# Transposing q of the last two batches by DMA instead of on the matrix engine, with a new order of units

## Chip, cores, metric

The kernel runs on one core of one Trainium2 chip. The metric is the device time of one execution in microseconds (us). Ratios below are between runs of the fast state alone. Medians and ranges are over all runs, slow ones included, as recorded; leaving out the slow ones moves no median by more than 0.2 us. A ratio is the mean time of one kernel's fast runs over the mean time of the fast runs of the kernel before in the same rounds on the same chip, so it is not quite the ratio of the medians that stand beside it.

Names: PE is the matrix engine (PEld its weight loads), DVE the vector engine, ACT the scalar engine, POOL GpSimd, SP the engine whose queue issues most stores and small copies. A profile line "L289" means line 289 of that kernel's source; the change shifts lines, so the q transposes are L289 before and L295 after, the spatial matmuls L473 and L494, the attends L381 and L402, the V projection L414 and L435, the output projection L514 and L535.

## The reference

Four batches, eight heads, 768 positions, head size 64. A small matrix per head mixes blocks of k and v; q, mixed k and mixed v go through attention inside blocks of 96; then a gated MLP with a spatial mixing matrix follows.

```
P      = five rounds of exp and row/column normalisation of sort_net     # [b, h, 8, 8]
k_sort = einsum('bhij,bhjcd->bhicd', P, k_blocks)                        # same for v
attn   = softmax(q_block @ k_sort_block.T / sqrt(64))                    # 96 x 96 per block
x      = attn @ v_sort_block                                             # heads side by side: [b, 768, 512]
h      = relu(x @ w_in);  u, v = halves of h
v_n    = layer-normalised v
gated  = u * (w_spatial @ v_n + b_spatial)
out    = gated @ w_out
```

## The kernel before

The whole program is a fixed list of short units, issued in list order on every engine. One token is a unit, its index, its batch, the engine that empties its PSUM tile (A for ACT, D for DVE), and which of four PSUM tiles it uses. `q11A2` is: transpose heads 4 to 7 of q of batch 1, in PSUM tile 2, copied out by ACT.

```python
UNITS = {"v": "vmix", "k": "ktr", "q": "qtr", "s": "score", "z": "sums", "a": "attend",
         "t": "vtr", "B": "vblk",
         "X": "vstart", "V": "vproj", "N": "norm", "U": "uproj", "S": "spatial", "O": "oproj"}
```

The q unit is 24 transposes on PE and one copy:

```python
def qtr(self, n, eng, ps):
    t = ps_tile(ps, BF16)
    qT = qk_pool.tile([128, 2, S], BF16, name="qT", tag="q", bufs=3)
    for x in range(2):
        hp = 2 * n + x
        for g in range(G):                       # G = 6
            for hh in range(2):
                nc.tensor.transpose(t[hh * 64:hh * 64 + 64, x, g * 128:(g + 1) * 128],
                    q_in[self.b][:, 2 * hp + hh, g * D:(g + 1) * D], ident_bf)
        self.q[hp] = qT[:, x, :].rearrange("p (g i t) -> p i g t", g=G, i=NB)
    copy(eng, qT, t[:, :, 0:S])
```

The v unit mixes v of one pair of heads. After both pairs of one half (heads 0 to 3, or 4 to 7) are done, eight small DMA copies bring that half into the block layout that the attends read. This part is not touched by the change, but the argument ends up here:

```python
def vmix(self, hp, eng, ps):
    # two matmuls into PSUM, copy to self.vm ... (cut)
    self.mixed.append(hp)
    if hp ^ 1 in self.mixed:                     # both pairs of this half are there
        for i in range(NB):                      # 8 copies of 48 KB on the SP queue
            nc.sync.dma_start(
                out=self.vb[:, i, half].rearrange("c h d -> c (h d)"),
                in_=self.vm[i * TB:(i + 1) * TB, half].rearrange("t g h d -> t g (h d)"))
```

The loads of batch b+1 are released by the first score of batch b, from GpSimd: v, then k, then q.

The softmax here doesn't subtract the row's maximum and nothing guards it: scores larger than these inputs give would overflow.

Of the kernel before, what the change touches and what calls it, by code (L numbers as in the profile page):

```python
# [9 lines left out]
BF16 = mybir.dt.bfloat16  # L10
# [6 lines left out]
def _raw_ap(base_ap: bass.AP, off_delta: int, dims) -> bass.AP:  # L17
    return bass.AP(
        tensor=base_ap.tensor,
        offset=base_ap.offset + off_delta,  # L20
        ap=[list(d) for d in dims],
    )
# [8 lines left out]
def kernel(  # L31
# [12 lines left out]
    nc = tc.nc  # L44

    B, H, S, D = q.shape
    NB = sort_net.shape[-1]
    BLK = S // NB
    G = S // 128
# [7 lines left out]
    HP = H // 2  # L57
# [5 lines left out]
    pd_pool = ctx.enter_context(tc.tile_pool(name="pd", bufs=B))  # L63
    ld = ctx.enter_context(tc.tile_pool(name="ld", bufs=2))
    att = ctx.enter_context(tc.tile_pool(name="att", bufs=2))
    qk_pool = ctx.enter_context(tc.tile_pool(name="qk", bufs=7))
    ex_pool = ctx.enter_context(tc.tile_pool(name="ex", bufs=8))
    xt_pool = ctx.enter_context(tc.tile_pool(name="xt", bufs=4))
    ln_pool = ctx.enter_context(tc.tile_pool(name="ln", bufs=3))
# [9 lines left out]
    def ps_tile(n, dt=FP32):  # L79
        return psum.tile(  # L80
            [128, 2, 512 if dt == FP32 else 1024], dt, name=f"ps{n}", tag=f"ps{n}",
        )
# [7 lines left out]
    b_nat = pers.tile([128, S], FP32)  # L90

    def load_heads(x, b, name):
        t = ld.tile([128, H, G * D], BF16, name=name, tag=name)
        nc.gpsimd.dma_start(  # L94
            out=t,
            in_=_raw_ap(x, b * H * S * D, [[G * D, 128], [S * D, H], [1, G * D]]),
        )
        return t

    v_in, k_in, q_in = {}, {}, {}  # L100
# [8 lines left out]
        out=a16.rearrange("p (j t) -> p j t", t=TB),  # L109
        in_=a16.rearrange("p (j t) -> p j t", t=TB),  # L110
# [6 lines left out]
        out=sel.rearrange("p i (j t) -> p i j t", t=TB),  # L117
        in_=sel.rearrange("p i (j t) -> p i j t", t=TB),
# [14 lines left out]
        out=w_in_sb.rearrange("p (j x) f -> p j (x f)", x=2),  # L133
        in_=moe_w_in.rearrange("(j p x) f -> p j (x f)", j=2, x=2),
# [20 lines left out]
    def sinkhorn():  # L155
        for n in range(5):
            nc.scalar.activation(out=p_all, in_=p_all, func=AF.Exp)
            nc.vector.reduce_sum(out=rowsum, in_=p_all, axis=AX.X)
            nc.vector.reciprocal(out=rowsum, in_=rowsum)
            nc.vector.tensor_mul(  # L160
                out=p_all, in0=p_all, in1=rowsum.to_broadcast([BH, NB, NB]),
            )
            nc.vector.reduce_sum(
                out=colsum, in_=p_all.rearrange("p i j -> p j i"), axis=AX.X,
            )
            nc.vector.reciprocal(out=colsum, in_=colsum)
            nc.vector.tensor_mul(
                out=p_all if n < 4 else p_bf, in0=p_all,
                in1=_raw_ap(colsum, 0, [colsum.ap[0], [0, NB], colsum.ap[1]]),
            )  # L170

    def warm(n, ps):
        t = ps_tile(ps)
        for _ in range(n):
            nc.tensor.matmul(t[:, 0, :], lhsT=ident_bf, rhs=warm_sb, start=True, stop=True)
# [5 lines left out]
    def make_pdiag(b, eng, h0, n, src=None):  # L181
        base = h0 if src is not None else b * NB * H + h0
        src = prep_sb if src is None else src
        eng.tensor_mul(
            out=pdiag[b][:, h0:h0 + n],
            in0=_raw_ap(mask16, 0, [mask16.ap[0], [0, n], [TB, NB], [1, TB]]),
            in1=_raw_ap(src, base, [src.ap[0], [1, n], [H, NB], [0, TB]]),
        )
# [5 lines left out]
    def transpose_p():  # L194
        for x in range(2):
            nc.vector.transpose(
                out=p_t[:, x, :], in_=p_bf[:, x * (NB // 2):(x + 1) * (NB // 2), :].rearrange("p i j -> p (i j)"),
            )
# [24 lines left out]
    def wsp_unit(gs, eng, ps):  # L223
        tp = ps_tile(ps, BF16)
        for go in range(G):
            nc.tensor.transpose(
                tp[:, 0, go * 128:(go + 1) * 128],
                wsp_nat[:, go, :].rearrange("p (s g) -> p g s", g=G)[:, gs, :],
                ident_bf,
            )  # L230
        copy(eng, wspT[:, gs, :], tp[:, 0, 0:S])

    def copy(eng, out, in_):
        if eng is nc.scalar:
            nc.scalar.copy(out=out, in_=in_)  # L235
        else:
            nc.vector.tensor_copy(out=out, in_=in_)
# [10 lines left out]
    class Attention:  # L248
# [7 lines left out]
        def vmix(self, hp, eng, ps):  # L256
# [18 lines left out]
            if hp ^ 1 in self.mixed:  # L275
                for i in range(NB):
# [2 lines left out]
                        in_=self.vm[i * TB:(i + 1) * TB, half].rearrange("t g h d -> t g (h d)"),  # L279
                    )  # L280

        def qtr(self, n, eng, ps):
            t = ps_tile(ps, BF16)
            qT = qk_pool.tile([128, 2, S], BF16, name="qT", tag="q", bufs=3)
            for x in range(2):
                hp = 2 * n + x
                for g in range(G):
                    for hh in range(2):
                        nc.tensor.transpose(  # L289
                            t[hh * 64:hh * 64 + 64, x, g * 128:(g + 1) * 128],  # L290
                            q_in[self.b][:, 2 * hp + hh, g * D:(g + 1) * D],
                            ident_bf,
                        )
                self.q[hp] = qT[:, x, :].rearrange("p (g i t) -> p i g t", g=G, i=NB)
            copy(eng, qT, t[:, :, 0:S])  # L295

        def mixed_t(self, src, hp, eng, ps):
            t = ps_tile(ps).rearrange("p x c -> p (x c)")
# [100 lines left out]
    class Gmlp:  # L399
# [122 lines left out]


    SCHEDULE = """
        k00A2 k10A3 k20D0 s10-1 s20-2 k30D3 s00-0 s30-1 t30D2 t10A3 t00D0 z10-1 t20D2 s40-3
        B10D1 B00D0 z00-2 B30D3 s60-1 a10-2 a00-0 B20D3 s50-1 s70-2 z20-1 X10-0 z30-3 a20-2
        a30-1 X00-3 V20-2 V10-- w30A1 V00-- U30A2 v11A0 v21A1 U20A3 w40D2 w10D0 N00-- U00A1
        v01A3 U10A2 w20D0 w50D1 w00A3 k11D2 k31A0 q01D1 k01A3 q11A2 k21A0 v31A1 S00-3 s01-2
        s11-0 S20-1 s51-3 s31-2 S10-0 z11-1 s21-3 S30-2 s61-1 a11-0 z01-3 a01-2 s71-1 s41-3
        O10D0 z31-1 z21-2 O00A3 a31-1 a21-0 O20D2 V01-3 v12D1 v02A0 V11-2 v32A3 V21-0 v22A2  # L530
        U01A1 k02A3 q12D0 k22A2 q02D1 k32A3 k12D0 U11D2 N01-- s42-1 s12-3 U21D0 s62-2 s02-1
        S01-3 s32-2 s72-1 S11-0 s52-3 s22-2 S21-1 z02-0 z22-3 U31D2 z32-0 a32-1 S31-3 a22-2
        z12-0 a12-1 a02-3 O21A0 O01D2 O11A1 V02-3 v13D0 v03A2 V12-1 v33A3 V22-2 v23A1 U02A0
        k03A3 q13D2 k23A1 q03D0 k33A3 k13D2 U12D1 N02-- s43-0 s13-3 U22D2 s63-1 s03-0 S02-3
        s33-1 s73-0 S12-2 s53-3 s23-1 S22-0 z03-2 z23-3 U32D1 z33-2 a33-0 S32-3 a23-1 z13-2  # L535
        a13-0 a03-3 O22A2 O02D1 O12A0 V03-3 V13-2 V23-1 N03-- U03A0 U13A3 U23A2 U33A1 S03-0
        S13-3 S23-2 S33-1 O03A0 O13A3 O23A2
    """
    UNITS = {
        "v": "vmix", "k": "ktr", "q": "qtr", "s": "score", "z": "sums", "a": "attend",  # L540
        "t": "vtr", "B": "vblk",
        "X": "vstart", "V": "vproj", "N": "norm", "U": "uproj", "S": "spatial", "O": "oproj",
    }
    with tc.manual_schedule(engines={ET.PE, ET.DVE, ET.Activation, ET.Pool}):
        attn = {b: Attention(b) for b in range(B)}
        gmlp = {}
        sinkhorn()
        warm(9, 1)
        attn[0].qtr(0, ACT, 2), attn[0].qtr(1, ACT, 3)
        warm(2, 1)  # L550
        transpose_p()
        spread(0, 1, 0), spread(1, 3, 1)
        for x in range(1, B):
            make_pdiag(x, nc.gpsimd, 0, H)
        nc.gpsimd.tensor_copy(
            out=b_bc.rearrange("p (g c) -> p g c", g=G),
            in_=b_nat.rearrange("p (c g) -> p g c", g=G),
        )
        for step in SCHEDULE.split():
            name, n, b = step[0], int(step[1]), int(step[2])  # L560
            eng = {"A": ACT, "D": DVE, "-": None}[step[3]]
            ps = None if step[4] == "-" else int(step[4])
            if name == "w":
                wsp_unit(n, eng, ps)
            elif name in "XVNUSO":
                if b not in gmlp:
                    gmlp[b] = Gmlp(b)
                if name == "S":
                    eng = DVE if b == B - 1 and len(gmlp[b].gt) == FC - 1 else nc.gpsimd
                getattr(gmlp[b], UNITS[name])(n, eng, ps)  # L570
            else:
                getattr(attn[b], UNITS[name])(n, eng, ps)
                if name == "s" and 1 <= b < B - 1 and len(attn[b].e) == 1:
                    gate = small.tile([1, 1], BF16, name="gate", tag="gate")
                    nc.gpsimd.tensor_copy(out=gate, in_=attn[b].e[n][0:1, 0, 0, 0:1])
                    v_in[b + 1] = load_heads(v, b + 1, "v_in")
                    k_in[b + 1] = load_heads(k, b + 1, "k_in")
                    q_in[b + 1] = load_heads(q, b + 1, "q_in")


# [28 lines left out]
```

## Time and profile before

| | kernel before |
|---|---|
| median, range | 158.89 us, 158.71 to 159.65 (3 runs) |
| profiled span, mean granted clock | 157.0 us, 0.998 |
| busy: PE, DVE, ACT, POOL | 142.9, 97.8, 92.4, 48.4 us |
| q units on PE | 8, of 24 transposes each |

PE is busy almost throughout. The measure that I use below is where the chain of PE work stands at fixed points: the start of the first q unit of batch 1, and the start of the first V unit of batches 1, 2 and 3 (V1, V2, V3). Between V1 and V2, and between V2 and V3, lies the same work of one whole batch, so the two distances are the price of a batch in PE time. Before they are 32.96 us each (V1 at 61.87, V2 at 94.83, V3 at 127.79 us). The lines of this profile that carry the bound stand in the prediction.

### The profile page before, as it was taken

To read this page: it belongs to the slowest core of one execution; us is meant where nothing else is said; L and a number is where in the kernel's file an instruction comes from. 1 tells how busy PE (TensorE), PEld (TensorE's weight loads), DVE (VectorE), ACT (ScalarE), POOL (GpSimd) and SP (SyncE) were. 2 spreads that over 40 slices of the span, in tenths; PEclk is the share of its full clock that TensorE was granted. 3 is DMA by queue.
4 is the path that set the end of the run, shared out by engine and by line. 5 is a ranking of instruction groups with operands and counts; after the bars stand their busy time and mean duration, and the time that the engine had idled before them with its cause. 6 is when DMAs were issued, how large, how long until landed. Compare 5 with 4: busy or idle time off the path is not lost.

```text
span 157.0 us, 4379 instructions
## 1 busy us (share of the span) xinstructions
PE 142.9 (91%) x1892; PEld 84.2 (54%) x1901; DVE 97.8 (62%) x197; ACT 92.4 (59%) x139; POOL 48.4 (31%) x47
## 2 busy tenths in 40 slices
PE   0967998979999999999999999999999999999960
PEld 0355884547865645467565544586556444666430
DVE  3777896487723566598944861999446837844510
ACT  3157977587894773597767326796564526640240
POOL 7975914000019920000757210000353400008400
PEclk9999999999999999999999999999999999999999
DMA  2999999999936999944599947045400063000064
GB/s 14 191 203 210 218 267 192 204 204 206 171 55 68 194 207 233 341 101 63 69 189 208 204 124 317 9 63 77 63 0 6 4 258 143 0 0 0 4 267 138
DMA packets 20964, 21.53 MB, mean 137 GB/s; under 512 B 1296, under 2 KB 18960, under 8 KB 20816
## 3 DMA queue, kind: packets, MB, share of 16 engines
q0 software_dynamic: 13504, 12.58, 49.8%
q1 hardware_dynamic: 7296, 8.53, 20.0%
q8 instruction: 15, 0.25, 0.6%
q10 hardware_dynamic: 144, 0.13, 0.3%
q14 instruction: 5, 0.04, 0.1%
HBM read 24.78 MB, written 6.29 MB: 198 GB/s over the span
## 4 chain that ended last, share of the span: by engine, by line
PE 66%; DMA 20%; POOL 5%; DVE 3%; issue 1%; POOLq 1%; DVEq 0%
DMA q_in<-in_q_dram 20%; PE ps L473 19%; PE ps L514 12%; PE ps L457 10%; PE ps L414 10%; PE ps L344 4%; PE ps L289 3%; DVE vs L484 2%; PE ps L301 2%; PE ps L381 2%; PE ps L260 2%; PE ps L363 1%; POOL v_in L94 1%; PE ps L500 1%; POOL k_in L94 1%
## 5 line engine op out<-in xcount | busy, mean ns | idle before, releaser
L485 POOL TENSOR_TENSOR gt<-vs,u_sb 128x768 bf16<-128x768 f32 x15 | 24.6, 1646 | 71.9 <-DVE vs L484 50.4
L473 PE MATMUL ps<-wspT,v_sb 128*128 128x384 bf16 x192 | 33.4, 327 | 0.0
L351 ACT ACTIVATE ex<-ps 96x768 bf16<-96x768 f32 x32 | 24.1, 803 | 9.5 <-PE ps L344 9.3
L484 DVE TENSOR_TENSOR vs<-ps,b_bc 128x768 f32<-128x768 f32 (+1 forms) x17 | 15.5, 911 | 21.0 <-PE ps L473 21.0
L473 PEld LDWEIGHTS <-v_sb 128*128 128x128 bf16 x192 | 17.9, 98 | 11.6
L457 PE MATMUL ps<-xt,w_in_sb 128*128 128x384 bf16 x128 | 23.0, 326 | 0.0
L436 DVE BATCH_NORM_STATS2 stats<-v_sb 128x6 f32<-128x512 bf16 x24 | 16.2, 674 | 10.1 <-ACT v_sb L241 10.1
L414 PE MATMUL ps<-w_in_sb,xt 128*128 128x512 bf16 x93 | 22.3, 379 | 0.2
L514 PE MATMUL ps<-w_out_sb,gt 128*128 128x512 bf16 x83 | 19.9, 380 | 0.4
L241 ACT ACTIVATE v_sb<-ps 128x1024 bf16<-128x1024 f32 (+1 forms) x15 | 12.4, 854 | 10.4 <-PE ps L414 10.4
L391 DVE TENSOR_TENSOR xt<-ps,lns 128x384 bf16<-128x384 f32 x32 | 15.7, 550 | 4.3 <-PE ps L381 3.3
L235 ACT COPY o_sb<-ps 128x1024 f32<-128x1024 f32 x7 | 7.1, 1012 | 18.0 <-PE ps L514 18.0
L457 PEld LDWEIGHTS <-w_in_sb 128*128 128x128 bf16 x128 | 12.0, 98 | 8.5 <-issue 0.6
L414 PEld LDWEIGHTS <-xt 128*128 128x128 bf16 x96 | 9.1, 98 | 10.6 <-DVE xt L391 0.4
L514 PEld LDWEIGHTS <-gt 128*128 128x128 bf16 x88 | 7.9, 98 | 10.3 <-POOL gt L485 1.2
L369 ACT ACTIVATE lns<-ps 128x384 f32<-128x384 f32 x16 | 7.8, 488 | 8.1 <-PE ps L363 8.0
L235 ACT CAST kT<-ps 128x768 bf16<-128x768 f32 x12 | 9.3, 803 | 1.8 <-PE ps L301 1.8
L344 PE MATMUL ps<-qT,kT 64*96 64x96 bf16 x256 | 9.7, 210 | 0.4 <-ACT kT L235 0.3
L344 PEld LDWEIGHTS <-kT 64*96 64x96 bf16 x256 | 7.2, 121 | 4.8 <-issue 3.7
L447 DVE TENSOR_SCALAR v_sb<-v_sb,mv,rstd 128x512 bf16<-128x512 bf16 x24 | 8.3, 417 | 0.6 <-ACT rstd L445 0.6
L370 ACT ACTIVATE lns<-lns 128x384 f32<-128x384 f32 x16 | 8.4, 523 | 0.5
L241 ACT ACTIVATE u_sb<-ps 128x768 bf16<-128x768 f32 x10 | 7.9, 811 | 1.2 <-PE ps L457 1.0
(78 smaller groups left out, 167.2 us busy)
## 6 DMA issues: line engine op xcount, KB each, us to landing
out_dram<-o_sb SPq DMA_DIRECT2D x11, 512.0 KB, 2.7
q_in<-in_q_dram POOLq DMA_DIRECT2D x4, 768.0 KB, 16.3
k_in<-in_k_dram POOLq DMA_DIRECT2D x4, 768.0 KB, 11.8
v_in<-in_v_dram POOLq DMA_DIRECT2D x4, 768.0 KB, 10.6
vb<-vm SPq DMA_DIRECT2D x48, 48.0 KB, 2.5
wsp_nat<-in_moe_w_spatial_dram POOLq DMA_DIRECT2D x1, 1152.0 KB, 21.6
w_in_sb<-in_moe_w_in_dram POOLq DMA_DIRECT2D x1, 1024.0 KB, 15.7
w_out_sb<-in_moe_w_out_dram POOLq DMA_DIRECT2D x1, 512.0 KB, 30.8
```

The costliest lines, as they stand in the source:

```text
L235: nc.scalar.copy(out=out, in_=in_)
L241: nc.scalar.activation(out=out, in_=in_, func=AF.Relu)
L344: nc.tensor.matmul(t[0:BLK, hh, ii * BLK:(ii + 1) * BLK], lhsT=self.k[hp][rows, i * BLK:(i + 1) * BLK], rhs=self.q[hp][rows, i], start=Tru ...
L351: nc.scalar.activation(out=e.rearrange("p h i c -> p h (i c)"), in_=t[0:BLK, :, 0:NB // 2 * BLK], func=AF.Exp, scale=scale,)
L391: nc.vector.tensor_mul(out=self.xt[j][:, dh, :].rearrange("p (g i t) -> p i g t", g=G, i=NB)[:, i0:i0 + NB // 2], in0=t[:, dh, 0:HW].rearr ...
L414: nc.tensor.matmul(self.vt[n][:, x, :], lhsT=self.xt(kc)[:, g * 128:(g + 1) * 128], rhs=w_in_sb[:, kc, DH:DFF], start=(kc == 0), stop=(kc ...
L436: nc.vector.bn_stats(out=stats, in_=v_sb[:, x, :])
L457: nc.tensor.matmul(t[:, x, 0:HW], lhsT=w_in_sb[:, kc, mc * 128:(mc + 1) * 128], rhs=self.xt(kc)[:, x * HW:(x + 1) * HW], start=(kc == 0), ...
L473: nc.tensor.matmul(t[:, x, 0:HW], lhsT=self.v[g][:, mc * 128:(mc + 1) * 128], rhs=wspT[:, g, x * HW:(x + 1) * HW], start=(g == 0), stop=(g ...
L484: nc.vector.tensor_add(out=vs[:, x], in0=t[:, x, 0:HW], in1=b2[:, x])
L485: eng.tensor_mul(out=gt2[:, x], in0=vs[:, x], in1=u2[:, x])
L514: nc.tensor.matmul(t[:, x, :], lhsT=self.gt[mc][:, g * 128:(g + 1) * 128], rhs=w_out_sb[:, mc, :], start=(mc == 0), stop=(mc == FC - 1),)
```

## The change

Intent: take the q transposes of batches 2 and 3 off PE. DVE puts q into pairs of heads in one copy, and one DMA on the SP queue transposes all 24 blocks of 128x128 a stage before they are needed. For this q of the next batch is loaded first, and the list of units was reordered. Some buffers changed too: q as loaded has one instead of two, and the transposed q lies in one tile for all four pairs of heads, with two buffers instead of three of half the size.

```diff
+        def qdma(self, n, eng, ps):
+            qr = qk_pool.tile([128, G, H, D], BF16, name="qr", tag="qr", bufs=1)
+            nc.vector.tensor_copy(
+                out=qr.rearrange("p g h d -> p h g d"),
+                in_=q_in[self.b].rearrange("p h (g d) -> p h g d", g=G),
+            )
+            nc.sync.dma_start(
+                out=self.q_tile().rearrange("p g x c -> p (g x) c"),
+                in_=qr.rearrange("p g h d -> p (g h d)"), transpose=True,
+            )
 ... (q_tile: one tile for the four pairs; qtr writes into it)
                     nc.gpsimd.tensor_copy(out=gate, in_=attn[b].e[n][0:1, 0, 0, 0:1])
+                    q_in[b + 1] = load_heads(q, b + 1, "q_in")
                     v_in[b + 1] = load_heads(v, b + 1, "v_in")
                     k_in[b + 1] = load_heads(k, b + 1, "k_in")
-                    q_in[b + 1] = load_heads(q, b + 1, "q_in")
```

The order, cut to batch 1 up to its first attends (before, then after):

```diff
-  V00-- U30A2 v11A0 v21A1 U20A3 w40D2 w10D0 N00-- U00A1 v01A3 U10A2 w20D0 w50D1 w00A3
-  k11D2 k31A0 q01D1 k01A3 q11A2 k21A0 v31A1 S00-3 s01-2 s11-0 S20-1 s51-3 s31-2 S10-0 z11-1
-  s21-3 S30-2 s61-1 a11-0 ...
+  V00-- v01A3 U20A1 v21D2 w20A0 N00-- U30A3 v31A1 U10A0 w30D2 w10A3 w00D1 v11A0
+  k01D2 k31A3 q01D1 k21A0 q11D2 k11D3 s01-1 S10-0 s71-2 s51-1 S20-3 s31-0 s61-2 S00-1 s11-3
+  s41-0 S30-2 s21-1 z11-3 Q02-- a11-0 ...
```

The new list moves two things that matter later. The v units stand in another order, and the first score of batch 1 (`s01`), which releases the loads of batch 2, now comes before the first spatial unit instead of after it.

Batches 2 and 3 are reordered likewise; the new unit `Q02` stands among the attends of batch 1, and `Q03` stands in batch 2 before its third spatial unit.

More of the change, by code (lines that the diff above doesn't have):

```diff
@@ L65 @@
     att = ctx.enter_context(tc.tile_pool(name="att", bufs=2))
-    qk_pool = ctx.enter_context(tc.tile_pool(name="qk", bufs=7))
+    qk_pool = ctx.enter_context(tc.tile_pool(name="qk", bufs=6))
     ex_pool = ctx.enter_context(tc.tile_pool(name="ex", bufs=8))
@@ L92, in load_heads @@
     def load_heads(x, b, name):
-        t = ld.tile([128, H, G * D], BF16, name=name, tag=name)
+        t = ld.tile([128, H, G * D], BF16, name=name, tag=name, bufs=1 if x is q else 2)
         nc.gpsimd.dma_start(
@@ L280, in vmix, with q_tile @@
                     )
+        def q_tile(self):
+            if not self.q:
+                qT = qk_pool.tile([128, G, HP, 128], BF16, name="qT", tag="q", bufs=2)
+                for hp in range(HP):
+                    self.q[hp] = qT[:, :, hp, :].rearrange("p g (i t) -> p i g t", i=NB)
+                self.qT = qT
+            return self.qT
         def qtr(self, n, eng, ps):
             t = ps_tile(ps, BF16)
-            qT = qk_pool.tile([128, 2, S], BF16, name="qT", tag="q", bufs=3)
             for x in range(2):
-                hp = 2 * n + x
                 for g in range(G):
@@ L290, in qtr @@
                             t[hh * 64:hh * 64 + 64, x, g * 128:(g + 1) * 128],
-                            q_in[self.b][:, 2 * hp + hh, g * D:(g + 1) * D],
+                            q_in[self.b][:, 4 * n + 2 * x + hh, g * D:(g + 1) * D],
                             ident_bf,
                         )
-                self.q[hp] = qT[:, x, :].rearrange("p (g i t) -> p i g t", g=G, i=NB)
-            copy(eng, qT, t[:, :, 0:S])
+            copy(
+                eng,
+                self.q_tile()[:, :, 2 * n:2 * n + 2, :].rearrange("p g x c -> p x g c"),
+                t[:, :, 0:S].rearrange("p x (g c) -> p x g c", g=G),
+            )
[8 more added lines that the diff above has]
+                in_=qr.rearrange("p g h d -> p (g h d)"), transpose=True,
+            )
         def mixed_t(self, src, hp, eng, ps):
@@ L524 @@
     SCHEDULE = """
-        k00A2 k10A3 k20D0 s10-1 s20-2 k30D3 s00-0 s30-1 t30D2 t10A3 t00D0 z10-1 t20D2 s40-3
-        B10D1 B00D0 z00-2 B30D3 s60-1 a10-2 a00-0 B20D3 s50-1 s70-2 z20-1 X10-0 z30-3 a20-2
-        a30-1 X00-3 V20-2 V10-- w30A1 V00-- U30A2 v11A0 v21A1 U20A3 w40D2 w10D0 N00-- U00A1
-        v01A3 U10A2 w20D0 w50D1 w00A3 k11D2 k31A0 q01D1 k01A3 q11A2 k21A0 v31A1 S00-3 s01-2
-        s11-0 S20-1 s51-3 s31-2 S10-0 z11-1 s21-3 S30-2 s61-1 a11-0 z01-3 a01-2 s71-1 s41-3
-        O10D0 z31-1 z21-2 O00A3 a31-1 a21-0 O20D2 V01-3 v12D1 v02A0 V11-2 v32A3 V21-0 v22A2
@@ L531 @@
-        U01A1 k02A3 q12D0 k22A2 q02D1 k32A3 k12D0 U11D2 N01-- s42-1 s12-3 U21D0 s62-2 s02-1
-        S01-3 s32-2 s72-1 S11-0 s52-3 s22-2 S21-1 z02-0 z22-3 U31D2 z32-0 a32-1 S31-3 a22-2
-        z12-0 a12-1 a02-3 O21A0 O01D2 O11A1 V02-3 v13D0 v03A2 V12-1 v33A3 V22-2 v23A1 U02A0
-        k03A3 q13D2 k23A1 q03D0 k33A3 k13D2 U12D1 N02-- s43-0 s13-3 U22D2 s63-1 s03-0 S02-3
-        s33-1 s73-0 S12-2 s53-3 s23-1 S22-0 z03-2 z23-3 U32D1 z33-2 a33-0 S32-3 a23-1 z13-2
-        a13-0 a03-3 O22A2 O02D1 O12A0 V03-3 V13-2 V23-1 N03-- U03A0 U13A3 U23A2 U33A1 S03-0
@@ L537 @@
-        S13-3 S23-2 S33-1 O03A0 O13A3 O23A2
+        k00A2 k10D3 k30D0 s00-1 s10-2 k20D3 s20-1 s30-0 t00D2 t10A3 t30D1 t20D0 z10-2 B00D3
+        s70-1 B10D2 s50-0 s40-3 z00-1 a10-2 a00-0 s60-3 B20D1 B30A2 z20-3 X10-0 z30-2 a20-1
+        a30-3 X00-2 V20-1 V10-- U00A3 w50A1 w40D0 V00-- v01A3 U20A1 v21D2 w20A0 N00-- U30A3
+        v31A1 U10A0 w30D2 w10A3 w00D1 v11A0 k01D2 k31A3 q01D1 k21A0 q11D2 k11D3 s01-1 S10-0
+        s71-2 s51-1 S20-3 s31-0 s61-2 S00-1 s11-3 s41-0 S30-2 s21-1 z11-3 Q02-- a11-0 z31-2
@@ new lines @@
+        z01-1 O10A3 a01-2 z21-0 O00A1 a21-3 a31-2 O20A0 V01-1 v32D3 V21-2 v22A0 U21A1 k12A2
+        v12A3 v02D0 V11-1 U31A2 k02A3 k22A0 k32D1 U01D2 N01-- s02-3 s52-0 U11A1 s72-2 s32-3
+        S21-0 s22-1 s42-2 S11-3 s62-0 s12-1 Q03-- S01-2 z32-3 z02-0 S31-1 z12-3 a02-2 a32-0
+        a12-3 O21A1 O11D2 z22-0 a22-3 O01A1 V02-0 v33D2 V22-3 v23A1 U22A0 k13A3 v13A2 v03D1
+        V12-0 U32A3 k03A2 k23A1 k33D0 U02D3 N02-- s03-2 s53-1 U12A0 s73-3 s33-2 S22-1 s23-0
+        s43-3 S12-2 s63-1 s13-0 S02-3 z33-2 z03-1 S32-0 z13-2 a03-3 a33-1 a13-2 O22A0 O12D3
@@ L538 @@
+        z23-1 a23-2 O02A0 V03-1 V13-3 V23-2 N03-- U03A0 U13A1 U23A3 U33A2 S03-0 S13-1 S23-3
+        S33-2 O03A0 O13A1 O23A3
     """
     UNITS = {
-        "v": "vmix", "k": "ktr", "q": "qtr", "s": "score", "z": "sums", "a": "attend",
+        "v": "vmix", "k": "ktr", "q": "qtr", "Q": "qdma", "s": "score", "z": "sums", "a": "attend",
         "t": "vtr", "B": "vblk",
```

## The prediction

> **What bounds the kernel now.** I read the page's busy shares and 40 slices first, then the waits of the matrix engine, then the chain of work that ended last inside one batch, then the transfers.
>
> ```profile
> PE 142.9 (91%) x1892; PEld 84.2 (54%) x1901; DVE 97.8 (62%) x197; ACT 92.4 (59%) x139; POOL 48.4 (31%) x47
> ...
> PE   0967998979999999999999999999999999999960
> DVE  3777896487723566598944861999446837844510
> PEclk9999999999999999999999999999999999999999
> ```
>
> PE is at nine tenths or more in almost every slice from 24 us to 149 us at full clock; the vector engine (DVE) has full slices only where a batch begins (slices 25 to 27, around 100 to 110 us). A high busy share alone proves little, because matmuls overlap, so the next view is what PE waited for over the whole span:
>
> ```profile
> PE ps L175 <- POOL ident_bf masks.py:199: 3.9, 1, 3.9
> PE ps L206 <- DVE mask L149: 1.4, 1, 1.4
> PE ps L260 <- DMA v_in<-in_v_dram: 0.8, 1, 0.8
> PE ps L363 <- ACT ex L351: 0.5, 1, 0.5
> PE ps L381 <- DVE vs L484: 0.5, 3, 0.2
> PE ps L289 <- DMA q_in<-in_q_dram: 0.5, 2, 0.3
> ```
>
> The two long ones are start-up. From 41 to 148 us PE waits about 0.7 us in total (L381 for DVE, L289 for q). So there its own instruction stream is the bound: taking PE work out pays in full, moving work between the other engines pays almost nothing. In the chain, for the opening of batch 2, the start-to-start costs can be read off:
>
> ```profile
> 69.81 0.46 PE ps L301 x12
> 70.27 0.67 PE ps L289 x24
> 70.94 0.34 PE ps L301 x12
> 71.27 0.67 PE ps L289 x24
> ...
> 76.40 2.06 PE ps L473 x12
> ```
>
> One q unit (L289, 24 transposes) holds PE 0.67 us, 28 ns per transpose; a spatial unit (L473) holds it 2.06 us. The 28 ns is what counts, not the 228 ns mean that the table of groups gives for one such instruction, since they are pipelined. Last, the front of the program:
>
> ```profile
> 9.91 30.90 DMA q_in<-in_q_dram
> 40.81 0.04 issue
> 40.85 0.86 PE ps L289 x24
> ```
>
> The q of batch 1 is requested at 9.91 us and lands at 40.8 us, behind 14 MB of other inputs read in the same queue. PE does not sit idle all that time, but no order of units can run this transpose earlier.
>
> **What the Trainium skill says.** "VectorE: DVE Perf Modes", section "The perf-mode tier table": a bf16 SBUF-to-SBUF copy of 2048 elements per partition takes 693 ns in the 4x mode. The kernel before has no such bf16 copy, so its trace neither agrees nor disagrees; the nearest rows are copies out of PSUM, 957 ns for 1536 elements. "DMA: Bandwidth & Descriptors", section "Latency and other measured facts": a DMA transpose was measured at 261 GB/s; no run shows one yet. The same page as the first, section "The three transpose paths", gives 1309 ns for one 128x128 block by DMA, which, if 24 blocks ran one after the other, would be 31 us; the two figures are an order of magnitude apart and I keep both as ends of a range. "SBUF — State Buffer", section "SBUF: two separate sides": DVE in a two-port mode and GpSimd hold one port pair exclusively, each for a whole instruction. The trace before has no clear case of it.
>
> **The change part by part.**
>
> Removed: four q units (two each in batches 2 and 3), 96 transposes on PE. 4 x 0.67 = 2.68 us of PE stream, all in the part where PE has nothing else to wait for: -2.7 us. With them go four PSUM-to-SBUF copies of q on DVE, 4 x 0.957 = 3.8 us, and four holdings of one of the four PSUM tiles; off the bound, worth nothing directly.
>
> Added on DVE: one copy of 128x3072 bf16 per batch. Estimate from the skill's 693 ns for 2048 elements in 4x mode, with 1024 more at 4 per cycle of 0.96 GHz (267 ns): 0.96 us. Two of them, 1.9 us, against 3.8 removed. If the strided output (64-element runs) drops it to 1x, about 3.3 us each.
>
> Added on the DMA: two transposes of 768 KB. At 261 GB/s 3.0 us plus some 2 us as the small stores before show (2.5 us to landing for 48 KB): 5 us. What they have: from the place of the new unit to the first scores of its batch PE must do, for batch 2, 4 attends (0.40 each), 3 sums (0.22), 3 output units (1.83), 3 V units (1.73), 3 U units (1.41), 4 v units (0.33) and 4 k units (0.34) = 19.9 us; for batch 3, about 24 us. A 5 to 15 us transpose is hidden.
>
> Moved, front: one batch-1 v unit (0.33 us) now stands ahead of the first batch-1 q unit instead of after the second. PE reaches that q unit just after or just before the data (it waits 0.15 us for it now, and 0.8 us for v earlier), so work pulled ahead of it fills idle time: -0.3 us.
>
> Moved, loads: q of the next batch goes first, then v, then k. In the kernel before, the three loads behind the gate landed 7.8, 11.6 and 17.6 us after their issues (batch 2) and 9.5, 11.9 and 15.0 (batch 3). So q lands 8 to 9.5 us after issue rather than 15 to 18. The new unit's DVE copy is in order with everything else on DVE, so it must not come up before that landing.
> Batch 2: gate opens about 1.3 us after the first score of batch 1 starts (PE 0.25, exp 0.8, gate 0.2); data at +9.3 to +11 us. Ahead of the copy PE has 4 spatial units (8.24) and 7 scores (0.245 each), and DVE one more 0.96 us add: +10.9. On time, or at worst barely late.
> Batch 3: ahead of the copy are only 2 spatial units (4.12), one U (1.41), 7 scores (1.7), less what follows the second spatial, plus the 0.96 us add: +7.8, against data at +9.2 to +11. DVE stands still 1.4 to 3 us. Behind it wait two spatial results and three attend results; I follow the four PSUM tiles: PE next needs the tile of the first late add about 2.7 us after DVE could have taken it, and the output units need the last spatial gate from GpSimd. I take 0.8 us of new PE waiting here, and 0.4 us around the batch-2 copy (its port conflict with GpSimd's 1.65 us multiply ahead of the output unit, and the 0.96 us it puts before the first attend result).
>
> Sum: -2.7 - 0.3 + 0.8 + 0.4 = -1.8; some of the 0.5 us that PE waited on L381 may go with the new order, -0.3. Together -2.1 to -2.3, from 158.89: **156.7 us**.
>
> **The rivals.**
> 1. Fully hidden. The q loads are in time and the order was tuned to these durations: -2.7 - 0.3 - 0.5 = -3.5, 155.4 us. For it: PE stays full in the old trace through equally crowded stretches. Against: the batch-3 sum above, and the 0.5 us cannot all be relied on.
> 2. The DVE copy blocks on the q load (or is a slow 1x copy of 3.3 us), and the PSUM tiles behind it run dry. DVE does 8.3 of 9 us of work from 69 to 78 us, but the new unit is placed earlier, where it does only 3.6 of 11 us (42 to 53). It would show 1 to 2.5 us of PE waits: 157.0 to 158.5 us.
> 3. The DMA transpose becomes the bound. Only if it takes more than about 18 us; at the 31 us of one-by-one blocks it would cost up to 12 us per batch, some 175 us. The bandwidth figure speaks against it, as does that the change gave it a whole stage of lead.
> 4. The transposes and stores delay the batch-2 v and k loads, which moved one place back. k then lands about 19.5 us after the gate; PE needs it at about +24. A delay of up to 4 us is free. Worth 0 to 1 us.
>
> **Range and chances.** The 2% line lies at 155.7 us, 3.2 us below. Removing PE work gives at most 2.7, so the line is crossed only if the moves also remove 0.5 us of the roughly 1.7 us of waits left after 20 us and add none: 0.18. Slower than 162.1 needs rival 3 or several faults at once: 0.04. Within 2%: 0.78. Range for 8 in 10: 155.2 to 158.2.
>
> **What would show it.** PE's L289 group goes from 192 to 96 instructions, busy PE drops some 3 us and its idle time after 41 us does not shrink. DVE's q copies go from 5 to 2 and the new copy lasts near 0.96 us. DVE's waits list the new copy waiting on the q load, in batch 3 above all, by 1 to 3 us; if there is none, rival 1 holds. The transpose lands within 15 us of issue, and no score waits for it; if one does, rival 3. The first batch-1 q unit still starts close to 41 us; if much earlier, my front is wrong. A span down by more than 3.2 us would mean that the new order removed waits I did not count.

## The result, and the profile after

The changed kernel took 157.28 us in the median of four runs (156.88 to 159.69; the 159.69 was in the slow state), the kernel before 158.80 us. The ratio of fast runs is 0.9886 (95% interval 0.984 to 0.993): about 1.1% faster, inside "within 2%". The profiled run was fast: 155.6 us of span.

First the busy shares and the row of PE by slice of the changed kernel, then what PE waited for (us in total, times, longest):

```profile
PE 141.0 (91%) x1792; PEld 81.9 (53%) x1805; DVE 94.3 (61%) x193; ACT 94.4 (61%) x141; POOL 49.0 (31%) x47
...
PE   0948999999999879999999999999999999999970
```

```profile
PE ps L175 <- POOL ident_bf masks.py:199: 3.9, 1, 3.9
PE ps L206 <- DVE mask L149: 1.6, 1, 1.6
PE ps L402 <- DMA vb<-vm: 1.6, 4, 0.4
PE ps L295 <- DMA q_in<-in_q_dram: 1.1, 1, 1.1
```

The third line is new. Slices 13 and 14 of PE (counted from 0; 51 to 58 us), full before, have an 8 and a 7. The attends of batch 1 wait for the block copies of v, which the prediction does not mention at all. The timeline of PE at that place (start, duration, what, idle time before it), the first attend of batch 1 in the kernel before and then in the changed one:

```profile
53.40 0.53 PE L381 MATMUL ps<-ex,vb 96*32 96x96 bf16 x32
```

```profile
53.31 0.35 PE L384 MATMUL ps<-ex,ones 96*32 96x384 bf16 x4
54.09 0.27 PE L402 MATMUL ps<-ex,vb 96*32 96x96 bf16 x8 [0.43 <-DMA vb<-vm]
54.77 0.27 PE L402 MATMUL ps<-ex,vb 96*32 96x96 bf16 x8 [0.41 <-DMA vb<-vm]
55.36 0.27 PE L402 MATMUL ps<-ex,vb 96*32 96x96 bf16 x8 [0.32 <-DMA vb<-vm]
56.04 0.27 PE L402 MATMUL ps<-ex,vb 96*32 96x96 bf16 x8 [0.41 <-DMA vb<-vm]
```

One attend of 32 matmuls is cut into four pieces of eight, each of which waits for one more copy to land. The loads that these copies meet start earlier than before, as POOL's small copy that releases them shows (before, then changed; the first load is issued at 48.36 and at 44.82 us):

```profile
48.24 0.18 POOL L575 COPY gate<-ex 1x1 bf16<-1x1 bf16 x1
```

```profile
44.30 0.18 POOL L596 COPY gate<-ex 1x1 bf16<-1x1 bf16 x1 [19.09 <-ACT ex L372]
```

The new unit itself did what was expected of it: the copy lasts about a microsecond, and nobody waited for the transpose. From the view of tile qr, the table of issues (last figure: median us to landing), and DVE's waits:

```profile
L309 DVE COPY qr<-q_in x2: 950/1011/1072, 54.1 to 85.2; 128x3072 bf16<-128x3072 bf16 x2
L313 SPq DMA_TRANSPOSE qT<-qr x2: 8469/8610/8750, 55.1 to 86.4; - x2
```

```profile
qT<-qr SPq DMA_TRANSPOSE x2, 12.3
```

```profile
DVE qr L309 <- DMA q_in<-in_q_dram: 1.5, 1, 1.5
```

Reading it by position of PE, all from the timelines of the profiled runs, in us:

| kernel | first q of batch 1 | q to V1 | V1 to V2 | V2 to V3 |
|---|---|---|---|---|
| before | 40.85 | 21.02 | 32.96 | 32.96 |
| changed | 40.88 | 22.50 | 31.83 | 31.82 |

Each full batch became 1.13 us cheaper, 2.27 us for two. The stretch from q to V1 became 1.48 us dearer, although it now holds 0.33 us less work (one v unit moved ahead of the q unit). PE therefore stands only 0.76 us ahead at V3, and from there to the start of the last group of output matmuls both kernels need 21.9 us. Another 0.6 us came after that: the span ends 7.3 us after that last group starts in the kernel before and 6.7 us in the changed one.

### The profile page after: what moved, and what is told of

The parts are those of the page before. It is cut to its first block, busy times and chain, and to the rows that moved or that the text cites. A ratio compares the mean times of both kernels' runs of the same rounds, so it can differ in the third digit from the quotient of the medians.

```text
span 155.6 us, 4192 instructions
## 1 busy us (share of the span) xinstructions
PE 141.0 (91%) x1792; PEld 81.9 (53%) x1805; DVE 94.3 (61%) x193; ACT 94.4 (61%) x141; POOL 49.0 (31%) x47
## 3 DMA queue, kind: packets, MB, share of 16 engines
q0 software_dynamic: 13504, 12.58, 50.3%
HBM read 24.78 MB, written 6.29 MB: 200 GB/s over the span
## 4 chain that ended last, share of the span: by engine, by line
PE 58%; DMA 10%; DVE 8%; ACT 7%; SPq 7%; POOL 3%; issue 3%; POOLq 1%; DVEq 0%
PE ps L435 13%; PE ps L478 12%; PE ps L535 10%; PE ps L494 9%; SPq L277 7%; DMA q_in<-in_q_dram 5%; DMA vb<-vm 4%; PE ps L322 4%; POOL gt L506 3%; ACT ex L372 3%; PE ps L260 2%; PE ps L365 2%; PE ps L402 2%; DVE vs L505 2%; PE ps L384 2%
## 5 line engine op out<-in xcount | busy, mean ns | idle before, releaser
L506 POOL TENSOR_TENSOR gt<-vs,u_sb 128x768 bf16<-128x768 f32 x15 | 25.2, 1688 | 49.9 <-DVE vs L505 26.3
L235 ACT COPY o_sb<-ps 128x1024 f32<-128x1024 f32 x9 | 9.1, 1012 | 18.2 <-PE ps L535 17.7
L241 ACT ACTIVATE u_sb<-ps 128x768 bf16<-128x768 f32 x14 | 11.1, 808 | 1.7 <-PE ps L478 1.2
L365 PEld LDWEIGHTS <-kT 64*96 64x96 bf16 x256 | 7.9, 129 | 4.7 <-issue 3.5
L237 DVE CAST kT<-ps 128x768 bf16<-128x768 f32 x10 | 9.2, 947 | 1.1 <-PE ps L322 1.1
L402 PE MATMUL ps<-ex,vb 96*32 96x96 bf16 x512 | 7.8, 207 | 1.7 <-DMA vb<-vm 1.6
```

The costliest lines, as they stand in the source:

```text
L241: nc.scalar.activation(out=out, in_=in_, func=AF.Relu)
L365: nc.tensor.matmul(t[0:BLK, hh, ii * BLK:(ii + 1) * BLK], lhsT=self.k[hp][rows, i * BLK:(i + 1) * BLK], rhs=self.q[hp][rows, i], start=Tru ...
L402: nc.tensor.matmul(t[c * DQ:(c + 1) * DQ, dh, ii * BLK:(ii + 1) * BLK], lhsT=self.vb[:, i, j, c, :].rearrange("c (d x) -> c x d", x=2)[:, ...
L506: eng.tensor_mul(out=gt2[:, x], in0=vs[:, x], in1=u2[:, x])
```

## The experiments

Theory V: what eats the gain is that the copies of half 0 of v land late. In the old list v units 1 and 0 (half 0) came before unit 3, so half 0 was copied first. In the new list the order is 0, 2, 3, 1: half 1 is complete first, its eight copies go first, and half 0, which the first attend reads, is issued last, when the loads of the next batch already run. In the kernel before the last copies met the loads too (five of them, in the window from 48 to 52 us, needed 4.5 us in the median), but they carried half 1, which is read from 59.33 us on and not from 53.40. Rival Q, from the prediction: the late q load and DVE's stall on it. Rival T: the DMA transpose crowds everything else. Twelve kernels were run, one of them the changed kernel once more; each was correct. Their positions, but for the fifth and the twelfth, are in one table after the sixth experiment.

**1. Half 0 first.** Only the places of v units 1 and 2 of batch 1 are exchanged.

```diff
-  v01A3 U20A1 v21D2 w20A0 ... w00D1 v11A0 k01D2
+  v01A3 U20A1 v11D2 w20A0 ... w00D1 v21A0 k01D2
```

> The changed kernel with one swap in the order of batch 1: v unit 1 takes the place of v unit 2 and the other way round, so that heads 0 to 3 (half 0), which the first attends read, go through the block copies of V first. Theory V (the lost time is the block copies of V that land last but are read first): PE's wait for the block copies, 1.6 us, is gone, the first V unit of batch 1 starts near 61.8 us instead of 63.4, and the time falls by 1.4 to 1.8 us, to about 0.978 of the kernel before. Theory Q (the late q load and DVE's stall on it are the loss, as predicted): no change in time, 0.989. Theory T (the DMA transpose slows everything around it): the wait moves or stays, time within 0.3 us.

Measured: 156.36 us (six runs, 155.71 to 156.75), ratio 0.9838 (0.981 to 0.987). The waits for the block copies are gone, although the loads are released as early as in the changed kernel (43.85 us), and q to V1 takes 21.20 us, 1.3 us less than there. Theory V holds, but the gain in time, 0.9 us by the medians, is less than I expected (against the changed kernel's repetition, experiment 10, the ratios differ by 0.9% or 1.4 us; the two rounds of that kernel differ by 0.6 us). A new wait shows why a part of it is missing:

```profile
PE ps L535 <- POOL gt L506: 0.4, 1, 0.4
```

and POOL's timeline of this run has two multiplies, one of them slow:

```profile
51.16 1.64 POOL L506 TENSOR_TENSOR gt<-vs,u_sb 128x768 bf16<-128x768 f32 x1 [0.82 <-DVE vs L505]
53.78 2.29 POOL L506 TENSOR_TENSOR gt<-vs,u_sb 128x768 bf16<-128x768 f32 x1 [0.97 <-DVE vs L505]
```

The slow one starts 0.16 us after DVE's pairing copy (53.62 to 54.57 us in this run) and takes 0.65 us longer; the output unit then waits 0.4 us for it. That is the conflict that the prediction put at 0.4 us with the batch-2 copy. In the changed kernel it was there too (a multiply of 2.29 us at 54.22) but lay behind the waits for the block copies.

**2. The batch-3 copy late.** `Q03` moves behind the last attend of batch 2.

```diff
-  s12-1 Q03-- S01-2 ... a12-3 O21A1
+  s12-1 S01-2 ... a12-3 Q03-- O21A1
```

> The changed kernel with the batch-3 pairing copy of q put after the last attend of batch 2 instead of before the third spatial unit. DVE's wait of 1.5 us for the q load should be gone in every theory. Theory Q (this stall costs PE 0.8 us, the prediction's term): the time falls by 0.6 to 1.0 us. Theory V (PSUM tiles and spare DVE time absorb it): it falls by 0.2 us at most, ratio 0.988 to 0.990.

Measured: 157.26 us (156.62 to 158.64), ratio 0.9918 (0.987 to 0.996). DVE no longer waits for q, and V1 to V2 is 31.83 us, the same as with DVE's stall of 1.5 us in it. So the stall cost PE nothing; rival Q falls. The ratio lies above what either theory gave, but within the scatter of the changed kernel (0.9925 in experiment 10). This run also shows that theory V's wait is a race: with the same instructions up to there, it was 0.7 us here instead of 1.6, with V1 0.9 us sooner after q.

**3. Old order, DMA transpose.** The old list with the four q units dropped, two Q units put in, and the PSUM tiles of a few k units renumbered.

```diff
-  U01A1 k02A3 q12D0 k22A2 q02D1 k32A3 k12D0 U11D2        # batch 3 likewise
+  U01A1 k02A3 k22A2 k32A0 k12D1 U11D2
-  O10D0 z31-1 ...  O21A0 O01D2
+  O10D0 Q02-- z31-1 ...  O21A0 Q03-- O01D2
```

> One part alone: the old order of units with q of batches 2 and 3 loaded first, paired by DVE and transposed by DMA, and the four q units dropped (PSUM tiles of a few k units renumbered, nothing else moved). If the removal of the PE transposes is worth its 2.7 us and the DMA transpose is hidden: 2.4 to 2.7 us faster than before, ratio 0.983 to 0.985, which is better than the whole change. If the new order is what makes the DMA transpose pay: slower than the changed kernel, above 0.990, with scores waiting for the transposed q or DVE waiting for the load.

Measured: 158.88 us (158.38 to 160.09), ratio 1.0004: no gain at all. I had expected 2.4 to 2.7 us. Two waits took it back:

```profile
PE ps L478 <- ACT kT L235: 1.7, 2, 0.9
...
PE ps L402 <- DMA vb<-vm: 1.1, 3, 0.4
```

The first is PSUM: with the q units gone, four k units follow one another in 1.55 us, and the next U unit waits for ACT to empty a tile, 0.87 us per batch. The second is the SP queue: in batch 2 the block copies of v begin at 69.26 us, directly after the transpose (59.43 to 68.05 us) and two stores, where the kernel before begins them at 67.46 us.

**4. The old order, spaced.** As the third, with a U unit between the k units.

```diff
-  U01A1 k02A3 k22A2 k32A0 k12D1 U11D2                    # batch 3 likewise
+  k02A3 U01A1 k22A2 k12D0 k32A3 U11D1                    # later tiles renumbered
```

> The old order with the DMA transpose, but with a U unit moved between the k units of batches 2 and 3, where the dropped q units had kept the copies of k on ACT apart. If the part alone gained nothing because four k units now follow one another faster than their PSUM tiles are emptied: the wait of 2 x 0.87 us is gone, 1.3 to 1.8 us faster than without it, ratio 0.989 to 0.993; what is left is the 1.1 us wait for block copies of V behind the DMA transpose in the same queue. If the loss is elsewhere: 0.998 or above.

Measured: 158.33 us (157.90 to 162.09, two of six runs slow), ratio 0.9957 (0.993 to 0.998). The PSUM wait is gone, and V2 to V3, which has no late block copies, fell from 32.56 to 31.85 us. But V1 to V2 stayed at 34.3 us: there the wait for block copies grew from 1.1 to 1.7 us. I had expected 0.989 to 0.993; half of the removed wait came back as a later one.

**5. New order, PE transposes.** The new list and load order, with the q units back on PE among the k units.

```diff
-  z11-3 Q02-- a11-0 ... k02A3 k22A0 k32D1 U01D2
+  z11-3 a11-0 ... k02A3 q02D0 k22A2 q12D1 k32D3 U01D0    # batch 3 likewise, later tiles renumbered
```

> The other part alone: the new order and the new load order, but q of batches 2 and 3 transposed on PE just before their first scores, as in the kernel before. Theory V: the new order itself loses 1.6 us at the block copies of V and gains 0.3 at the front, so about 1.3 to 1.7 us slower than before, ratio 1.008 to 1.011, with the wait for the block copies in its trace although there is no DMA transpose. Theory T: no wait for the block copies here, and the ratio is 0.996 to 1.000.

Measured: 160.67 us (160.31 to 162.76), ratio 1.0116 (1.008 to 1.015). The profiled run was in the slow state, so I read only the list of waits of it here (more in experiment 10): 1.6 us for the block copies, with no DMA transpose in the program. The order alone makes that wait; rival T falls as its cause.

```profile
PE ps L402 <- DMA vb<-vm: 1.6, 4, 0.7
```

**6. The same with half 0 first.** The fifth kernel with the exchange of the first experiment.

> New order with v units 1 and 2 of batch 1 swapped, and q of batches 2 and 3 transposed on PE, so without any DMA transpose and without waits for the block copies. If a q unit is worth its 0.67 us of PE stream and nothing else is at play: 2.7 us slower than the best kernel so far (155.3), so 157.9 to 158.3 us, ratio 0.994 to 0.998, and the stretch from the first V unit of batch 2 to that of batch 3 is 33.2 us against 31.8. If the earlier kernel with PE transposes was slow for another reason than the block copies: above 1.005.

Measured: 158.73 us (158.46 to 159.18), ratio 0.9999, all runs fast. Against the fifth kernel the exchange alone is worth 1.2% here, where no DMA transpose is about. Against the best kernel (below) a batch costs 33.18 us instead of 31.82: 1.36 us for two q units, 0.68 each. The total distance, 3.4 us by the medians, is 0.7 us more than these 2.7; of that, some 0.6 us lies in the last stores, as the twelfth experiment takes up. So my range of 157.9 to 158.3 us missed.

All positions (us, profiled runs; the fifth kernel is left out, its profile being slow; experiments 7 to 11 follow below):

| kernel | first q of batch 1 | q to V1 | V1 to V2 | V2 to V3 |
|---|---|---|---|---|
| half 0 first (1) | 40.44 | 21.20 | 31.90 | 31.83 |
| batch-3 copy late (2) | 41.00 | 21.61 | 31.83 | 31.82 |
| old order, DMA (3) | 40.96 | 21.01 | 34.26 | 32.56 |
| old order, spaced (4) | 40.85 | 21.01 | 34.30 | 31.85 |
| half 0 first, PE transposes (6) | 41.25 | 20.59 | 33.18 | 33.19 |
| loads released later (7) | 40.78 | 21.45 | 34.54 | 31.83 |
| both moves (8) | 40.87 | 21.21 | 31.83 | 31.83 |
| three moves (9) | 40.65 | 20.59 | 31.82 | 31.82 |
| changed again (10) | 40.76 | 23.46 | 31.83 | 31.83 |
| transpose twice (11) | 40.87 | 21.79 | 33.91 | 31.83 |

**7. Loads released later.** The list of v units as in the change; the loads of batch 2 are released by the fifth score of batch 1 instead of the first, and the batch-2 copy follows later.

```diff
-                if name == "s" and 1 <= b < B - 1 and len(attn[b].e) == 1:
+                if name == "s" and 1 <= b < B - 1 and len(attn[b].e) == (5 if b == 1 else 1):
-  z11-3 Q02-- a11-0 z31-2 z01-1 O10A3 a01-2 z21-0
+  z11-3 a11-0 z31-2 z01-1 O10A3 a01-2 Q02-- z21-0
```

> Order of the v units as in the change, but the q, v and k loads of batch 2 are released by the fifth score of batch 1 instead of the first (some 5 us later), with the batch-2 pairing copy after the second attend. If the block copies of V land late because the loads crowd the DMA engines: the last lands about 2.5 us after its issue instead of 6 us, PE's wait for them falls from 1.6 us to under 0.4 us, and the time is 1 us or more below the changed kernel unless k of batch 2 now comes late. If they are late only because they are issued last in a row of 0.6 us each: the wait stays at 1 us or more.

Measured: no wait for block copies. The line of the block copies in the table of issues, for those issued between 42.5 and 51 us, in the changed kernel and then in this one (count, KB each, median us to landing):

```profile
vb<-vm SPq DMA_DIRECT2D x10, 48.0 KB, 6.3
```

```profile
vb<-vm SPq DMA_DIRECT2D x11, 48.0 KB, 2.2
```

So the same copies, issued at the same time and in the same order, need 2.2 us alone and 6.3 us beside the loads: the lateness is their being issued last together with the traffic they meet there. Together with experiment 1: without either of the two, the place or the traffic, the wait is gone. The time is no better, though: 160.02 us, ratio 1.0086. As the expectation left open, k of batch 2 now comes late (1.5 us of PE waiting), DVE waits 2.8 us for q of batch 3, and output units wait. Releasing the loads this much later (gate at 50.55 us) is the wrong remedy; ordering the copies is the right one.

**8. Both moves.** The first and second experiments together.

> The swap of v units and the late batch-3 copy together, the batch-2 copy left where the change has it. Theory V: the late batch-3 copy adds nothing (0 to 0.2 us) to the swap, ratio 0.981 to 0.984. Theory Q: another 0.6 us or more, 0.980 or below.

Measured: 156.05 us (155.72 to 156.50), ratio 0.9828 (0.980 to 0.985). Against the exchange alone 0.3 us by the medians, within the scatter; the output unit still waits 0.4 us for the slow multiply.

**9. Three moves.** In addition the batch-2 copy goes behind the second attend of batch 1, away from POOL's multiply.

```diff
-  z11-3 Q02-- a11-0 z31-2 z01-1 O10A3 a01-2 z21-0
+  z11-3 a11-0 z31-2 z01-1 O10A3 a01-2 Q02-- z21-0
```

> The changed kernel with all that the traces point to: v units 1 and 2 of batch 1 swapped, the batch-3 pairing copy after the last attend of batch 2, and the batch-2 pairing copy after the second attend of batch 1, so that it no longer runs beside GpSimd's last multiply (2.29 us beside the copy, 1.64 us otherwise, and the output unit waited 0.45 us for it). If the waits for the block copies and for that multiply are the whole of the loss, PE reaches the first V unit of batch 1 near 61.2 us and the time is about 2.0 to 2.3 us below the changed kernel, ratio to the kernel before 0.975 to 0.978. If the multiply wait was covered by another: 0.980 to 0.984, as with the swap alone.

Measured: 155.34 us (155.11 to 155.85), ratio 0.9786 (0.976 to 0.981), the fastest of all and narrower in its scatter than the changed kernel. It beats both kernels. No wait for block copies or for the multiply stands in PE's list, and q to V1 is 20.59 us, as in the sixth kernel, which has no DMA transpose. The batch-3 transpose, which now runs when the loads have all but landed, is issued in 3.56 us instead of 8.75 (SP's timeline of this run) and lands 5.5 us after its issue instead of 12.2:

```profile
58.86 5.08 SPq L313 DMA_TRANSPOSE qT<-qr  x1
...
90.38 3.56 SPq L313 DMA_TRANSPOSE qT<-qr  x1
```

**10. The changed kernel again**, for its scatter.

> The changed kernel once more, beside the others on the same chip: ratio 0.987 to 0.991, and a wait for the block copies of V between 0.7 and 1.7 us in the profile, different from the first one[...].

Measured: 158.24 us (156.38 to 158.96, one slow run), ratio 0.9925 (0.988 to 0.997); the ratio is a little outside what I expected. The wait was 1.0 us, but q to V1 was 23.46 us, almost 1 us more than in the first profile with its 1.6 us of waits. The windows from 52 to 60 us show where the rest lies (after the five engines: granted clock, DMA share, GB/s):

```profile
52.00:54.00 2.00, 1.68 (x30) 0.88 (x30) 0.93 (x2) 0.96 (x2) 1.13 (x1) 1.00 1.27 214
54.00:56.00 2.00, 1.28 (x33) 0.55 (x34) 1.25 (x3) 1.29 (x4) 1.89 (x1) 0.98 1.33 207
56.00:58.00 2.00, 2.00 (x6) 0.76 (x5) 0.66 (x2) 1.65 (x4) 0.40 (x1) 0.50 1.30 205
58.00:60.00 2.00, 2.00 (x40) 0.72 (x39) 0.11 (x1) 0.69 (x1) 0.00 (x0) 0.67 1.31 196
```

Right after the pieces of waiting, the granted clock is a half for about 3.4 us (0.08 of the second window, all of the third, 1.3 of the fourth). Half of 3.4 us is 1.7 us lost, on top of 1.0 us of waiting: together about the 2.87 us by which this q to V1 exceeds the 20.59 us of the kernel without such waits (experiment 9). The first profile of the changed kernel had the waits without a half-clock stretch there (it had one near 14 to 17 us, before the load-bound q unit, which still started at 40.88 us). So q to V1 is 1.3 to 2.3 us longer than with half 0 first (21.20 us), profile by profile, which fits the wide scatter of this kernel. That the short waits bring on the half clock is my inference from its place; no run here was built to test it, and the traces speak on both sides. The profile of the fifth kernel has the same stretch in the same place, from 56.44 to 59.85 us after 1.6 us of such waits; its q to V1 is 24.07 us against 20.59 in the sixth, and its two full batches are as there (33.19 and 33.18 us). But the fourth kernel has four waits of the same kind, 1.7 us in all, between 84.5 and 87.1 us, and the clock stays full after them. What decides it stays open.

**11. Transpose twice.** Each transpose is issued a second time into the same place.

```diff
-            nc.sync.dma_start(out=self.q_tile()..., in_=qr..., transpose=True)
+            for _ in range(2):
+                nc.sync.dma_start(out=self.q_tile()..., in_=qr..., transpose=True)
```

> The changed kernel with each DMA transpose issued twice, the second into the same place after the first has landed. If the transpose is hidden with the lead the traces show (some 8 us before the first score of batch 2, some 8 to 9 before that of batch 3): the second landing, 20 to 25 us after the first issue, comes 0 to 5 us too late in each batch, so scores wait, and the time rises by 2 to 9 us, ratio 1.00 to 1.045. If the transpose already cost time by crowding the DMA engines, loads of v and k would be waited for as well.

Measured: 159.04 us (four runs, 158.63 to 159.60), ratio 1.0020. No score waited for q even now, so the transpose has ample lead. The 1.8 us above the changed kernel's first median came another way: the second transpose holds the SP queue, so the block copies of v of batch 2 start at 72.05 us instead of 69.10, land late, and V1 to V2 grows by 2.1 us. SP's timeline:

```profile
55.07 8.55 SPq L314 DMA_TRANSPOSE qT<-qr  x1
63.72 0.51 SPq L543 DMA_DIRECT2D out_dram<-o_sb  x1
67.26 3.58 SPq L314 DMA_TRANSPOSE qT<-qr  x1
70.94 1.01 SPq L543 DMA_DIRECT2D out_dram<-o_sb  x2
72.05 12.46 SPq L277 DMA_DIRECT2D vb<-vm  x16
```

The cost of a DMA transpose in this kernel is thus not the wait for its result but what stands behind it in its queue.

**12. Two more DMAs.** The kernel before with two small loads added to the SP queue at the start, to see where the 0.6 us at the end come from.

```diff
+    for n in range(2):
+        spare = pers.tile([BH, NB, NB], FP32, ...)
+        nc.sync.dma_start(out=spare, in_=sort_net.rearrange("b h i j -> (b h) i j"))
```

> The kernel before, unchanged but for two more small loads on the SP queue at the start, whose data nothing reads. In all ten profiles of kernels with two DMA transposes the span ends 6.6 to 6.7 us after the last group of output matmuls starts; in the three without them, 7.3 us. If that comes from the SP queue having two more DMAs (the place of the last stores in the row shifts by two): 6.7 us here too, and about 0.6 us faster than before, ratio 0.996. If it comes from the transposes themselves or from the new copies: 7.3 us and a ratio of 1.000.

Measured: 158.68 us, ratio 0.9977 (0.995 to 1.0005): unclear. The end is 7.2 us after the last group starts (149.25 to 156.4), between the two values. The first of the last small stores is issued 1.73 us after that start, as in the changed kernel (1.72), and not 2.08 as before; the last of them has landed 5.4 us after it, against 5.3 in the changed kernel and 5.9 before. But from that landing to the end of the span it takes 1.8 us here and 1.4 us in the other two. So the two DMAs bring the landings forward, and most of that does not reach the end; why stays open.

## Why the prediction was right, and where not

The measured 157.28 us lies in the range of 155.2 to 158.2 and within 2%, as forecast with a chance of 0.78. The total is right partly because two terms were wrong in opposite directions.

- **Removed PE work, -2.7 us: right.** Two batches cost 33.18 us each with q on PE and 31.82 without (experiments 6 and 9): 2.7 us. Against the kernel before only 2.27 us shows, because the new order with q on PE costs 33.18 per batch, 0.22 more than the old one's 32.96. The prediction did not charge the order for that, and no run shows where it goes.
- **Front, -0.3 us: right in size.** The q unit starts at 40.88 us as before, bound by the load, and the moved v unit leaves 0.33 us less after it.
- **DVE copy, 0.96 us: right.** 0.95 and 1.07 us; the strided output did not drop it to a slower mode. Rival 2 in its slow-copy form is out.
- **DMA transpose, 5 us, hidden: hidden, but mis-sized.** It took 12.3 us to land and held the SP queue for 8.6 us while the loads ran; the estimate fits only a transpose that has the DMA engines nearly to itself (5.5 us, experiment 9). Rival 3 is out; the doubled transpose delayed no score either. What the prediction did not see is the queue behind it (experiments 3, 4, 11).
- **q lands 8 to 9.5 us after its issue: right** (8.3 and 7.8 us). **DVE stalls 1.4 to 3 us at the batch-3 copy: right** (1.5 us). **That costs PE 0.8 us: wrong.** Moving the copy away changed nothing (31.83 both times). I followed the PSUM tiles by hand and put each delay on PE; in the trace DVE is idle again for 0.7 us from 87.2 us, right behind the copy and the late add, and PE's list of waits from 64 us to the end of its work is empty.
- **0.4 us around the batch-2 copy: right in mechanism and size,** 0.65 us on the multiply and 0.4 us on PE, but hidden in the changed kernel behind a larger wait. Together with its place before the attends, moving it was worth 0.6 us between q and V1 (21.21 to 20.59).
- **The missing term.** Nothing in the sum stands for the block copies of v: 1.6 us of PE waits in the first profile, and 1.3 us and more between q and V1. The old trace had the number: 48 copies in the table of issues, landing after 2.2 us at best and 7.4 us at worst. I compared the two lists for their q units and loads, and did not ask of the other moved units which later unit reads them. The v units' order 0, 2, 3, 1 against the old 1, 2, 0, 3 is visible in the diff, and so is the earlier first score, which releases the loads 3.5 us sooner, into these copies.
- **The waits on L381, -0.3 us:** gone from the list indeed, though the new order cost 0.22 us per batch, as said above.
- **The end, -0.6 us:** not predicted, and only partly explained.
- **Slips of reading, on which the sum does not rest:** the eight loads ahead of that q in its queue come to about 13 MB read (an estimate: 6.4 MB in the table of issues, and the page has 24.78 MB read for the 12.58 MB of that queue), not 14 MB; slices 5, 17 and 19 of DVE's row are full too, not only 25 to 27; PE's waits after 20 us add up to 2.0 us, not 1.7.

Rival 1, everything hidden, at 155.4 us, describes not the changed kernel but the one with three moves, at 155.34 us. Rival 4 did not come about: neither v nor k of batch 2 was waited for in the changed kernel. It came about at once when the loads were released some 6 us later (experiment 7).

## What to carry to other kernels

Where one engine's stream is the bound, work taken off it can pay in full (1.36 us per batch for two q units here), but removing units from a hand-made order also removes the spacing they gave to others: the part alone, in the old order, gained nothing. After a reorder, follow every small copy to its first reader, and issue first what is read first, before large loads enter the same DMA engines. A DMA that is hidden itself can still cost time through whatever stands behind it in its queue.

## What the Trainium skill lacked or had wrong

- "DMA: Bandwidth & Descriptors", section "Latency and other measured facts", has 261 GB/s for a DMA transpose. Here 768 KB landed after 12.3 us beside running loads (64 GB/s with all latency in it) and after 5.5 us without them (143 GB/s). Apart from a vendor's cycle count for earlier generations it has no time for how long a transpose holds the issuing queue: 7.6 to 9.5 us beside loads, 5.1 us while the last load ended and 3.5 to 3.6 us otherwise.
- "VectorE: DVE Perf Modes", section "The three transpose paths": its 1309 ns per block would be 31 us for 24 blocks in a row (an estimate); the DMA of 24 blocks took 5.5 to 12.3 us. The 4x copy time of 693 ns for 2048 elements in its section "The perf-mode tier table" agrees: 0.95 us for 3072 elements.
- "DMA: Bandwidth & Descriptors", section "Issuing engines are not separate DMA queues", says that DMAs of different issuers interleave on the same engines. It agrees, but has no size for it: copies of 48 KB from SP landed after 2.2 us alone and 6.3 us beside GpSimd's loads.
- "SBUF — State Buffer", section "SBUF: two separate sides": the exclusive port pair fits what is seen; a GpSimd multiply of 1.64 us took 2.29 us when it began 0.16 us into a 0.95 us DVE copy.
- "TensorE: Matmul & The Clock Gate", section "What's actually happening", gives the half clock after an idle window of about 3.4 us. Here half-clock stretches of 3.4 us came although PE was not idle: in the 3.4 us before them it was busy for 2.38 us (changed kernel, second profile) and 1.92 us (fifth kernel). And they did not come after 3.4 us with 1.95 us of busy PE (seventh kernel, from 66.95 us) or 2.14 us (fourth kernel, from 85.0 us).
